# Attention scores from two float32r products on full stacks, with q and k loaded in token order

## The chip, the core and the metric

The program runs on one core of a Trainium2 chip. Its time is device time in microseconds (us), the median of several executions. The core has five engines with queues of their own: TensorE (PE, with its weight loads shown as PEld), VectorE (DVE), ScalarE (ACT), GpSimd (POOL) and SyncE (SP), which issues nearly all transfers here. Engines wait for each other by semaphores only; within an engine instructions go in the order in which they were issued.

## What is computed

Causal attention with a decay, over 4 batches of 8 heads, 576 tokens and 64 columns per head, then two feed-forward blocks over the 2304 tokens of width 512, with 2048 hidden columns each:

```python
log_f = np.log(np.clip(f, 0.0001, 1.0))
cum = np.cumsum(log_f, axis=-1)
scores = q @ k.T / sqrt(64) + cum[:, None] - cum[None, :]   # above the diagonal: -1e9
attn = exp(scores - max) ; attn = attn / (sum(attn) + 1e-9)
x = attn @ v                                    # heads side by side: 2304 x 512
h = x @ w_in  ; x = (h * tanh(softplus(h))) @ w_out          # first block
h = x @ w_in2 ; out = (h * cos(h)) @ w_out2                   # second block
```

The weights come as float64 and are cut into two float32r parts (`hi`, `lo`) on the chip; the feed-forward products take three float32r matmuls each (x high by weight high, x high by weight low, x low by weight high).

## The kernel before

**Attention.** The heads go in pairs, 16 of them: `jobs`. A pair of batch 0 is two jobs (query blocks 0 and 1, then 2 to 4), so batch 0 has eight small jobs; each pair of batches 1 to 3 is one full job of five blocks, twelve in all. A full job's blocks have 64, 128, 128, 128 and 128 query rows, and the keys seen by them (`w`) are 64, 192, 320, 448 and 576; the last is cut at 384, so that its products are 384 and 192 wide.

`load_job` (L401) loads q and k of a pair, a DMA each, so that one partition holds `C` neighbouring tokens. `prep_job` (L435) makes a *stack* of them: it transposes pieces of at most 96 tokens on TensorE (L462) into a bank of PSUM, and copies these to the stack by `ScalarE` (L474, both heads of k and the second head of q) and `VectorE` (L476, the first head of q). The copies write every `C`th column, which puts tokens back into order. A stack is `[128, head, q or k, token]` in float32: 64 rows of q or k, a row of the running sum `cum` and rows of 1 and -1, so that one product of 128 rows gives score plus decay. There are two stacks in a ring (`stk0`, `stk1`): the next job's is made in the last half-steps of the current job, from half-step `begin` on.

`scores` (L482) runs one float32 product for each head and cut (L491), and then on VectorE the mask and the row maximum in one reduction (L519), on ScalarE the exponential (L524); `normalise` (L530) divides on GpSimd (L538). Three blocks later `transposes` turns the result on TensorE (L565, L581) and `av` multiplies with v (L603) and cuts x into two float32r parts (L618, L619). The block of 64 rows holds both heads side by side, 64 columns of TensorE each, with a mask of its own (`mask2`).

**Feed-forward.** From the second batch on, steps of the first feed-forward pass (half of the hidden columns, tiles of 256 tokens, L205 and L227) are issued between the half-steps of attention. Behind attention come the rest of that pass, the other half of the columns and the second block, on tiles of 384 tokens.

**Order.** The text of the program gives priorities; the order on each engine is then made by a scheduler with a model of the chip before the program is compiled. Tiles of a tag are given out in turn from a pool with `bufs` buffers, and the taker of one waits until its last user is done.

Of the kernel before, what the change touches and what calls it, by code (L numbers as in the profile page):

```python
# [9 lines left out]
F32 = mybir.dt.float32  # L10
# [26 lines left out]
def tile_attention_two_ffn(  # L37
# [31 lines left out]
    rawp = ctx.enter_context(tc.tile_pool(name="raw", bufs=3))  # L69
# [3 lines left out]
    mask2 = const.tile([128, 320], F32, name="mask2")  # L73
# [6 lines left out]
    cumd = dram.tile([B * H, S], F32, name="cumd")  # L80
# [7 lines left out]
    def split_weights(layer, chunks, pool, slot0=0):  # L88
# [11 lines left out]
        def load(i):  # L100
            if i < len(pieces):
                c, nm, nb, nn, src, per, u, slot = pieces[i]
                raws[i] = rawp.tile([128, per, nn, 2], I32, tag="raw", name="raw")
                nc.sync.dma_start(out=raws[i].rearrange("p b n t -> p b (n t)"), in_=src[:, u : u + per])

        PF = 2
# [37 lines left out]
    def ffn_units(passes, p, hbank, abank, ready):  # L144
# [12 lines left out]
        def load_x(ti):  # L157
# [8 lines left out]
            t = p.tile([128, 2, NK, TB], F32R, tag="x", name="x")[:, :, :, 0:T]  # L166
# [126 lines left out]
        def v_1(n):  # L293
# [3 lines left out]
            t = tmp("n", n)  # L297
# [86 lines left out]
    def attention_units(p, bank):  # L384
# [16 lines left out]
        def load_job(jb):  # L401
# [32 lines left out]

        def prep_job(jb):  # L435
# [6 lines left out]
            src = cums[0][h0 : h0 + 2] if jb == 0 else cumd[h0 : h0 + 2]  # L442
            nc.sync.dma_start(out=st[96:97, :, 0], in_=src)
            nc.sync.dma_start(out=st[64:65, :, 1], in_=src)
# [14 lines left out]
            for g in groups:  # L459
# [3 lines left out]
                for which, lo in ((0, qlo), (1, 0)):  # L463
# [18 lines left out]
        def scores(jb, i):  # L482
# [352 lines left out]
```

## Time and profile before

| | us |
|---|---|
| median of the runs (3) | 1109.8 |
| lowest, highest | 1107.9, 1110.19 |
| the profiled execution | 1108.41 |
| its span | 1106.6 |
| TensorE busy | 1066.5 (96%) |
| VectorE busy | 642.2 (58%) |
| ScalarE busy | 588.6 (53%) |
| GpSimd busy | 230.4 (21%) |
| score products, L491 | 115.1 of records, 384 of them |

The mean granted clock was 0.991. Attention takes roughly the first 400 us, and the share of TensorE that is busy is lowest in the first slices of the span. Busy time of a matmul record includes its way through the array, so the sum of a line's records is more than the time for which the line holds TensorE; the distance between starts tells that. Rows are named `engine line out<-in`; `128x448` is partitions by elements.

### The profile page before, as it was taken

The page shows a single profiled execution, that of the slowest core. Times are in us where ns is not written, and L with a number is a line of the kernel's source. Part 1 is how long each engine was busy: PE and PEld are TensorE (multiplying, and loading weights), DVE is VectorE, ACT ScalarE, POOL GpSimd, SP SyncE. Part 2 cuts the span into 40 slices and gives each one's busy share as a digit, 9 for nine tenths or more (in the row PEclk, how much of TensorE's full clock was granted, in tenths as well). Part 3 has the DMA queues.
Part 4 walks back from the last instruction along what each step waited for, and adds up shares of the span by engine and source line. Part 5 has one row for each costly group of instructions (what it writes and reads, how often), then busy time and mean ns, then how long its engine had stood idle before and what let it go on. Part 6 is the DMA issues. An engine that isn't in the chain of part 4 may idle for free.

```text
span 1106.6 us, 17736 instructions
## 1 busy us (share of the span) xinstructions
PE 1066.5 (96%) x6496; PEld 936.6 (85%) x6496; DVE 642.2 (58%) x1461; ACT 588.6 (53%) x1196; POOL 230.4 (21%) x267
## 2 busy tenths in 40 slices
PE   5888999899999999999999999999999999999998
PEld 4565787578877879999999999879999999999997
DVE  6768775576656566453555625996445454454543
ACT  5776776767767655443444424665334343343433
POOL 6545632232322323130111101230000000000000
PEclk9899999999999999999999999999999999999999
DMA  7744622442232127463455544542001020100000
GB/s 163 183 122 126 196 55 74 110 130 54 74 91 93 33 73 228 158 210 114 158 190 185 168 153 142 172 134 67 20 30 57 1 86 1 58 29 1 30 1 29
DMA packets 118807, 110.53 MB, mean 100 GB/s; under 512 B 64560, under 2 KB 100912, under 8 KB 118720
## 3 DMA queue, kind: packets, MB, share of 16 engines
q1 hardware_dynamic: 118720, 109.40, 32.5%
q8 instruction: 51, 0.84, 0.3%
q14 instruction: 36, 0.29, 0.1%
HBM read 80.99 MB, written 28.39 MB: 99 GB/s over the span
## 4 chain that ended last, share of the span: by engine, by line
PE 83%; DVE 7%; ACT 5%; issue 3%; POOL 1%; DMA 1%; SPq 0%; ACTq 0%; POOLq 0%; DVEq 0%
PE h L205 19%; PE acc L236 17%; PE acc L227 16%; PE hx L205 14%; PE s L491 7%; PE s L603 5%; PE s L581 4%; ACT stk L474 3%; PE s L462 1%; DVE raw L123 1%; DVE raw L124 1%; DVE raw L133 1%; DVE s L519 1%; ACT s L524 1%; DMA raw<-in_moe_w_in_dram 0%
## 5 line engine op out<-in xcount | busy, mean ns | idle before, releaser
L205 PE MATMUL h<-x,wih 128*128 128x384 f32 (+1 forms) x1056 | 242.6, 317 | 0.0
L343 DVE TENSOR_TENSOR gl<-e,gh 128x384 fp32r<-128x384 f32 (+1 forms) x157 | 108.8, 693 | 142.5 <-ACT gh L335 142.5
L205 PEld LDWEIGHTS h<-x,wih 128*128 128x128 f32 x1056 | 180.9, 189 | 8.9 <-issue 2.8
L205 PE MATMUL h<-x,wil 128*128 128x384 f32 (+1 forms) x528 | 167.5, 317 | 0.0
L205 PE MATMUL hx<-x,wih 128*128 128x384 f32 (+1 forms) x672 | 166.2, 328 | 0.0
L335 ACT ACTIVATE gh<-e 128x384 fp32r<-128x384 f32 (+1 forms) x180 | 97.9, 545 | 100.6 <-DVE e L331 53.8
L227 PE MATMUL acc<-gl,woh 128*128 128x256 f32 (+1 forms) x480 | 148.9, 311 | 0.0
L227 PE MATMUL acc<-gh,woh 128*128 128x256 f32 (+1 forms) x480 | 148.5, 312 | 0.1
L227 PE MATMUL acc<-gh,wol 128*128 128x256 f32 (+1 forms) x480 | 147.5, 308 | 0.0
L491 PE MATMUL s<-stk 128*128 128x192 f32 (+7 forms) x384 | 115.1, 426 | 15.2 <-ACT stk L474 6.3
L538 POOL TENSOR_SCALAR s<-s,sm 128x448 f32<-128x448 f32 (+5 forms) x144 | 90.8, 645 | 159.7 <-DVE sm L536 50.4
L205 PEld LDWEIGHTS hx<-x,wih 128*128 128x128 f32 x672 | 120.1, 188 | 4.2
L236 PE MATMUL acc<-woh,gl 128*128 128x512 f32 x288 | 113.3, 397 | 3.1 <-DVE gl L343 3.1
L236 PE MATMUL acc<-wol,gh 128*128 128x512 f32 x288 | 113.7, 395 | 0.0
L236 PE MATMUL acc<-woh,gh 128*128 128x512 f32 x288 | 112.3, 390 | 0.8 <-DVE part L272 0.8
L205 PE MATMUL hx<-x,wil 128*128 128x384 f32 (+1 forms) x336 | 110.4, 328 | 0.0
L524 ACT ACTIVATE s<-s,mx 128x448 f32<-128x448 f32 (+5 forms) x144 | 83.1, 578 | 41.6 <-DVE mx L519 40.9
L205 PEld LDWEIGHTS h<-x,wil 128*128 128x128 f32 x528 | 99.8, 189 | 1.3 <-issue 0.6
L316 ACT ACTIVATE n<-n 128x384 f32<-128x384 f32 x96 | 50.4, 525 | 87.1 <-DVE n L305 87.1
L227 PEld LDWEIGHTS acc<-gh,woh 128*128 128x128 f32 x480 | 90.7, 190 | 2.8 <-issue 1.1
L227 PEld LDWEIGHTS acc<-gl,woh 128*128 128x128 f32 x480 | 90.9, 189 | 2.1 <-issue 0.7
L227 PEld LDWEIGHTS acc<-gh,wol 128*128 128x128 f32 x480 | 91.0, 190 | 2.0 <-issue 1.1
(88 smaller groups left out, 1705.0 us busy)
## 6 DMA issues: line engine op xcount, KB each, us to landing
raw<-in_moe_w_in_dram SPq DMA_DIRECT2D x32, 512.0 KB
raw<-in_moe_w_out_dram SPq DMA_DIRECT2D x32, 512.0 KB
x<-xd SPq DMA_DIRECT2D x6, 1536.0 KB
x<-yd SPq DMA_DIRECT2D x6, 1536.0 KB
x<-xd SPq DMA_DIRECT2D x8, 1024.0 KB
xd<-xs SPq DMA_DIRECT2D x12, 576.0 KB
natk<-in_k_dram SPq DMA_DIRECT2D x16, 288.0 KB
pd<-part SPq DMA_DIRECT2D x18, 256.0 KB
```

The lines of the kernel that those rows point to most:

```text
L205: nc.tensor.matmul(o, lhsT=a[wsl], rhs=b[:, kk, :], start=(kk == 0 and i == 0), stop=(kk == NK - 1 and i == 2),)
L227: nc.tensor.matmul(o, lhsT=a[dsl], rhs=b[:, gs], start=(start and i == 0 and d % nsub == 0), stop=(end and i == 2), skip_group_check=True,)
L236: nc.tensor.matmul(acc[ti][m], lhsT=a[:, ms], rhs=b[:, j, :], start=(start and i == 0), stop=(end and i == 2),)
L316: nc.scalar.activation(out=t, in_=t, func=AF.Sin, scale=TWO_PI)
L335: nc.scalar.activation(out=gh, in_=e, func=AF.Copy)
L343: marks["v1"] = nc.vector.tensor_tensor(out=gl, in0=st[n][0], in1=f(gst[n][0]), op=ALU.subtract)
L474: nc.scalar.activation(out=o, in_=i_, func=AF.Copy, scale=sc)
L491: marks["score"] = nc.tensor.matmul(o, lhsT=st[:, j, 0, qs], rhs=st[:, j, 1, c0:c1], start=True, stop=True)
L524: nc.scalar.activation(out=s[:, 0:w], in_=s[:, 0:w], func=AF.Exp, scale=-1.0, bias=mx, accum_out=sm[:, j : j + 1])
L538: nc.gpsimd.tensor_scalar(out=s[:, 0:w], in0=s[:, 0:w], scalar1=sm[:, j : j + 1], scalar2=1.0, op0=ALU.mult, op1=ALU.mult)
L581: nc.tensor.transpose(t[:, 128 * x : 128 * x + 128], ss[j][:, QS[c] : QS[c] + 128], ident)
L603: nc.tensor.matmul(t[64 * j : 64 * j + 64, c0:width], lhsT=vt[jb][0:kr, c, j], rhs=pt[0:kr, j, c, c0:width], start=(c == 0), stop=(c == nb ...
```

## The change

The stacks become float32r and have room for two parts, `x` = 0 and 1: `[128, q or k, x, head, token]`. Part 0 has 128 rows: the high part of q (or k) in rows 0 to 63 and, in rows 64 to 127, for q the high part again, for k the low part. Part 1 has 68 rows: for q the low part, for k the high part again, and four rows of ones and of `cum`, which is itself stored in two parts. Each score is the sum of two products in PSUM, one per part (L524).

Each piece in PSUM is now written to the stack four times by three engines: ScalarE writes the high part (L501), VectorE the low part as the piece times its scale less the high part (L502), and the high part again goes by ScalarE for the first head of q (L506) or by GpSimd from the stack (L508). q and k are loaded so that one partition holds every 96th token (two DMAs each, L417), so the pieces are contiguous in the stack; only job 0 keeps the old order. The block of 64 rows takes a product of 128 columns for each head, and its reduction is split in two (L560). The stacks take more room, which is found by fewer buffers: `raw` 2 (was 3), q and k 3 together (was 4), `n` 2 (was 3), the feed-forward's x tiles of 256 and of 384 tokens in tiles of their own. The preparation begins one half-step earlier.

```diff
@@ load_job
-                t = p.tile([128, 6, 2, D], F32, tag=f"nat{nm}", name=f"nat{nm}", bufs=2)
-                nc.sync.dma_start(out=t[0:P, 0:C], in_=src[b, hs, lo:khi].rearrange("h (p c) d -> p c h d", c=C))
+                t = p.tile([128, 6, 2, D], F32, tag="nat", name=f"nat{nm}", bufs=3)
+                if jb == 0:
...
+                else:
+                    for j in range(2):
+                        nc.sync.dma_start(
+                            out=t[0:P, 0:C, j], in_=src[b, 2 * hp + j, lo:khi].rearrange("(c p) d -> p c d", c=C)
+                        )
@@ prep_job
+                    sc = 0.125 if which == 0 else 1.0
                     for j in range(2):
-                        o = st[0:64, j, which, lo:khi].rearrange("r (p c) -> r c p", c=C)[:, c0 : c0 + n]
-                        i_ = t[64 * j : 64 * j + 64, at : at + n * P].rearrange("r (c p) -> r c p", p=P)
-                        sc = 0.125 if which == 0 else 1.0
-                        if which or j:
-                            nc.scalar.activation(out=o, in_=i_, func=AF.Copy, scale=sc)
+                        i_ = t[HALVES[j], at : at + n * P]
+                        if jb == 0:
+                            i_ = i_.rearrange("r (c p) -> r c p", p=P)
+
+                        def o(x, rows):
...
+                            return st[rows, which, x, j, lo + c0 * P : lo + (c0 + n) * P]
+
+                        again, low = (o(0, bottom), o(1, top)) if which == 0 else (o(1, top), o(0, bottom))
+                        nc.scalar.activation(out=o(0, top), in_=i_, func=AF.Copy, scale=sc)
+                        nc.vector.scalar_tensor_tensor(
+                            out=low, in0=i_, scalar=sc, in1=f(o(0, top)), op0=ALU.mult, op1=ALU.subtract
+                        )
+                        if which == 0 and j == 0:
+                            nc.scalar.activation(out=again, in_=i_, func=AF.Copy, scale=sc)
                         else:
-                            nc.vector.tensor_scalar(out=o, in0=i_, scalar1=sc, scalar2=None, op0=ALU.mult)
+                            nc.gpsimd.tensor_copy(again, f(o(0, top)))
@@ scores
-            def product(o, j, c0, c1):
-                marks["score"] = nc.tensor.matmul(
-                    o, lhsT=st[:, j, 0, qs], rhs=st[:, j, 1, c0:c1], start=True, stop=True
-                )
+            def product(o, j, c0, c1, cols=qs):
+                for x, rows in ((0, slice(0, 128)), (1, slice(0, 68))):
+                    marks["score"] = nc.tensor.matmul(
+                        o, lhsT=wide(st, rows, x, j, cols), rhs=st[rows, 1, x, j, c0:c1],
+                        start=x == 0, stop=x == 1,
+                    )
...
             if r == 64:
-                t = bank()[:, 0:w]
+                t, parts = None, []
                 for j in range(2):
-                    product(t[64 * j : 64 * j + 64], j, 0, w)
-                heads.append([(t, 0, w, mask2[:, 320 - w : 320])])
+                    if t is None or 2 * w > 512:
+                        t = bank()
+                    o = t[:, j * w : j * w + w] if 2 * w <= 512 else t[:, 0:w]
+                    product(o, j, 0, w, slice(QS[i] - 64 * j, QS[i] - 64 * j + 128))
+                    end = S - 64 + 64 * j
+                    parts.append((o, 0, w, maskt[:, end - w : end], HALVES[j]))
+                heads.append(parts)
@@ attention_units
-            ring.append(p.tile([128, 2, 2, S], F32, name=f"stk{i}", bufs=1))
+            ring.append(p.tile([128, 2, 2, 2, S], F32R, name=f"stk{i}", bufs=1))
...
-                begin = max(0, 2 * len(bl) - 5)
+                begin = max(0, 2 * len(bl) - 6)
```

On TensorE, before, the end of the sixth full job stands like this (`stk_99` is the stack in use, `stk_115` the next job's; `x2` counts like instructions in a row):

```order
L491 MATMUL s_2415<-stk_99 128x448
L491 MATMUL s_2417<-stk_99 128x448
L603 MATMUL s_2427<-p,natv 64x256 x8
L603 MATMUL s_2427<-p,natv 64x128 x2
L462 MATMUL s_2441<-ident,natq 128x96 x5
L565 MATMUL s_2474<-ident,s 64x128
L462 MATMUL s_2481<-ident,natq 128x96
L462 MATMUL s_2481<-ident,natk 128x96 x4
L491 MATMUL s_2506<-stk_99 128x384
L491 MATMUL s_2508<-stk_99 128x384
L491 MATMUL s_2510<-stk_99 128x192 x2
L462 MATMUL s_2525<-ident,natk 128x96 x2
```

The same place after the change (`stk_101` in use, `stk_108` the next):

```order
L482 MATMUL s_2710<-ident,natq 128x96 x5
L524 MATMUL s_2723<-stk_101 128x448 x2
L524 MATMUL s_2726<-stk_101 128x448 x2
L644 MATMUL s_2737<-p,natv 64x256 x8
L644 MATMUL s_2737<-p,natv 64x128 x2
L482 MATMUL s_2751<-ident,natq 128x96
L482 MATMUL s_2751<-ident,natk 128x96 x4
L606 MATMUL s_2794<-ident,s 64x128
L482 MATMUL s_2801<-ident,natk 128x96 x2
L524 MATMUL s_2825<-stk_101 128x384 x2
L524 MATMUL s_2828<-stk_101 128x384 x2
L524 MATMUL s_2831<-stk_101 128x192 x4
```

The first five transposes of q now stand ahead of the products of width 448, and the last two of k ahead of those of width 384 and 192, where they stood behind them; each product is two.

On ScalarE the evacuation of that job stood, before, as one run:

```order
L524 ACTIVATE s,sm<-s,mx 128x448 x2
L618 ACTIVATE xs<-s_2427 128x256
L474 ACTIVATE stk_115<-s_2441 64x5x96
L474 ACTIVATE stk_115<-s_2481 64x96
L474 ACTIVATE stk_115<-s_2481 64x4x96 x2
L474 ACTIVATE stk_115<-s_2525 64x2x96 x2
L524 ACTIVATE s,sm<-s,mx 128x576
```

After, exponentials (L565), a part of x (L659) and a copy of transposed rows (L598) stand between its pieces:

```order
L501 ACTIVATE stk_108<-s_2710 64x480
L659 ACTIVATE xs<-s_2737 128x256
L501 ACTIVATE stk_108<-s_2751 64x96
L501 ACTIVATE stk_108<-s_2801 64x192
L506 ACTIVATE stk_108<-s_2751 64x96
L501 ACTIVATE stk_108<-s_2751 64x96
L501 ACTIVATE stk_108<-s_2801 64x192
L501 ACTIVATE stk_108<-s_2751 64x384
L598 ACTIVATE p<-s_2858 128x2x2x128
L565 ACTIVATE s,sm<-s,mx 128x576
L501 ACTIVATE stk_108<-s_2751 64x384
L565 ACTIVATE s,sm<-s,mx 128x576
```

The six copies became nine, one of which stands ahead of these rows, and the next exponential of a whole row (128x576) stands between the last two of them.

On GpSimd, the divisions (L579, L538 before) of that stretch have the new copies among them:

```order
L508 CAST stk_108<-stk_108 64x480
L579 TENSOR_SCALAR s<-s,sm 128x448 x2
L508 CAST stk_108<-stk_108 64x96
L508 CAST stk_108<-stk_108 64x384
L508 CAST stk_108<-stk_108 64x192
L508 CAST stk_108<-stk_108 64x384
L508 CAST stk_108<-stk_108 64x192
L579 TENSOR_SCALAR s<-s,sm 128x576 x2
```

Before, that engine had only L538 and L341 there; now the last four copies of k go behind the division of the 448 wide block and ahead of that of 576.

## Rows read from the trace of the kernel before

**Rows 1.** Time by stage: PE, PEld, DVE, ACT, POOL busy (instructions), clock, DMA share, GB/s.

```profile
0.00:130.00 130.00, 105.71 (x663) 74.40 (x664) 97.31 (x267) 89.36 (x199) 78.68 (x99) 0.93 0.59 153
130.00:400.00 270.00, 262.75 (x1892) 207.70 (x1891) 166.95 (x532) 188.70 (x429) 80.56 (x117) 1.00 0.30 84
440.00:480.00 40.00, 40.00 (x335) 40.00 (x335) 19.61 (x30) 18.77 (x31) 11.25 (x8) 1.00 0.51 167
520.00:560.00 40.00, 40.00 (x232) 40.00 (x232) 20.72 (x32) 17.21 (x34) 5.42 (x5) 1.00 0.58 190
80.00:120.00 40.00, 36.43 (x248) 26.16 (x247) 35.49 (x88) 27.86 (x64) 27.05 (x26) 0.96 0.50 142
```

**Rows 2.** Instructions by line, L491: busy us, mean ns, idle before; then min/median/max ns.

```profile
L491 PE MATMUL s<-stk 128*128 128x448 f32 x64 | 30.6, 586 | 0.0
L491 PE MATMUL s<-stk 128*128 128x384 f32 x64 | 25.8, 501 | 2.9 <-ACT stk L474 0.9 <-DVE p L559 0.9 <-DVE xs L619 0.8
L491 PE MATMUL s<-stk 128*128 128x192 f32 x112 | 23.4, 332 | 0.1
...
L491 PE MATMUL s<-stk x384: 222/432/955, 9.3 to 393.8; 128*128 128x192 f32 x56, 128*128 128x448 f32 x32, 128*128 128x384 f32 x32, 128*64 128x64 f32 x24
```

**Rows 3.** Timeline of TensorE around L491: start us, busy us, work.

```profile
323.01 2.10 PE L491 MATMUL s<-stk 128*128 128x384 f32 x8
324.95 0.33 PE L462 MATMUL s<-ident,natk 96*128 96x96 f32 x2
...
334.75 1.67 PE L491 MATMUL s<-stk 128*128 128x448 f32 x4
336.35 0.65 PE L603 MATMUL s<-p,natv 64*64 64x256 f32 x4
```

**Rows 4.** Timeline at 321 us: TensorE's weight loads for L462.

```profile
321.03 0.45 PEld L462 LDWEIGHTS s<-ident,natq 96*128 96x128 f32 x5 [0.17 <-issue]
```

**Rows 5.** Groups by line and shape: VectorE, ScalarE, GpSimd (busy us, mean ns, idle before).

```profile
L476 DVE TENSOR_SCALAR stk<-s 64x480 f32<-64x480 f32 x12 | 12.4, 1037 | 0.5 <-PE s L462 0.5
...
L331 DVE SCALAR_TENSOR_TENSOR e<-n,h 128x384 f32<-128x384 f32 x48 | 26.5, 553 | 25.5 <-ACT n L316 25.5
...
L519 DVE CUSTOM_DVE_ANT_0 s<-s,maskt 128x192 f32<-128x192 f32 x24 | 7.5, 351 | 0.0
...
L474 ACT ACTIVATE stk<-s 64x480 f32<-64x480 f32 x12 | 12.7, 1062 | 10.7 <-DVE stk L476 10.7
...
L474 ACT ACTIVATE stk<-s 64x192 f32<-64x192 f32 x32 | 16.6, 520 | 1.8 <-PE s L462 1.3
...
L284 ACT ACTIVATE e<-h 128x384 f32<-128x384 f32 x24 | 11.7, 488 | 15.8 <-PE h L205 15.6
...
L284 ACT ACTIVATE e<-h 128x512 f32<-128x512 f32 x7 | 4.1, 589 | 3.2 <-PE h L205 3.2
...
L538 POOL TENSOR_SCALAR s<-s,sm 128x448 f32<-128x448 f32 x32 | 22.4, 711 | 32.3 <-DVE sm L536 21.8 <-PE s L462 9.7 <-PE s L581 0.8
...
L538 POOL TENSOR_SCALAR s<-s,sm 128x192 f32<-128x192 f32 x24 | 11.9, 507 | 2.5 <-ACT e L314 1.1 <-DVE sm L536 1.0 <-ACT p L557 0.3
```

**Rows 6.** TensorE's waits, 130 to 400 us; chain of waits, 195 to 203 us.

```profile
PE s L491 <- ACT stk L474: 2.3, 4, 0.9
...
by line: ACT stk L474 44.1%; PE s L603 16.5%; DVE stk L476 11.6%; PE s L581 8.4%; issue 7.3%; DVE xs L619 5.3%; ACT xs L618 4.9%; PE s L491 4.2%
```

**Rows 7.** Timeline at 99 us; L299 on VectorE by itself (min/median/max ns).

```profile
99.22 1.39 POOL L138 TENSOR_TENSOR wol<-raw,woh 128x512 fp32r<-128x512 f32 x1 [0.30 <-ACT woh L137]
...
99.38 0.32 DVE L476 TENSOR_SCALAR stk<-s 64x96 f32<-64x96 f32 x1
...
99.54 1.35 DVE L299 TENSOR_SCALAR n<-e 128x512 f32<-128x512 f32 x1
...
L299 DVE TENSOR_SCALAR n<-e x23: 408/427/1387, 61.1 to 412.0; 128x512 f32<-128x512 f32 x23
```

More of the change, by code (lines that the diff above doesn't have):

```diff
@@ L68, in tile_attention_two_ffn @@
     w0p = ctx.enter_context(tc.tile_pool(name="w0", bufs=1))
-    rawp = ctx.enter_context(tc.tile_pool(name="raw", bufs=3))
+    rawp = ctx.enter_context(tc.tile_pool(name="raw", bufs=2))
     ident = const.tile([128, 128], F32, name="ident")
     maskt = const.tile([128, S], F32, name="maskt")
-    mask2 = const.tile([128, 320], F32, name="mask2")
     two = const.tile([128, 1], F32, name="two")
@@ L79, in tile_attention_two_ffn @@
     pd = dram.tile([128, NK, NT], F32, name="pd")
-    cumd = dram.tile([B * H, S], F32, name="cumd")
+    cumd = dram.tile([B * H, 2, S], F32, name="cumd")
     W = {}
@@ L102, in load @@
                 c, nm, nb, nn, src, per, u, slot = pieces[i]
-                raws[i] = rawp.tile([128, per, nn, 2], I32, tag="raw", name="raw")
+                pl, nbuf = (late[0], 1) if late and i % 3 > 1 else (rawp, 2)
+                raws[i] = pl.tile([128, per, nn, 2], I32, tag="raw", name="raw", bufs=nbuf)
                 nc.sync.dma_start(out=raws[i].rearrange("p b n t -> p b (n t)"), in_=src[:, u : u + per])
-        PF = 2
+        PF = 2 if late else 1
         with tc.issue_after(marks["cum"].ins):
@@ L165, in load_x @@
             src = xd if tl["layer"] == 1 else yd
-            t = p.tile([128, 2, NK, TB], F32R, tag="x", name="x")[:, :, :, 0:T]
+            if attention_over:
+                t = late[0].tile([128, 2, NK, TB], F32R, tag="x", name="x", bufs=2)[:, :, :, 0:T]
+            else:
+                t = ap.tile([128, 2, NK, TA], F32R, tag="xa", name="xa", bufs=2)
             nc.sync.dma_start(
@@ L441, in prep_job @@
             h0 = b * H + 2 * hp
-            src = cums[0][h0 : h0 + 2] if jb == 0 else cumd[h0 : h0 + 2]
-            nc.sync.dma_start(out=st[96:97, :, 0], in_=src)
-            nc.sync.dma_start(out=st[64:65, :, 1], in_=src)
+            top, bottom = HALVES
+            for which, rows, lo in ((0, slice(64, 66), qlo), (1, slice(66, 68), 0)):
+                if jb == 0:
+                    for j in range(2):
+                        nc.sync.dma_start(
+                            out=f(st[rows, which, 1, j, lo:khi]), in_=cums[0][h0 + j : h0 + j + 1, :, lo:khi]
+                        )
+                else:
+                    nc.sync.dma_start(
+                        out=f(st[rows, which, 1, :, lo:khi]),
+                        in_=cumd[h0 : h0 + 2, :, lo:khi].rearrange("j x s -> x j s"),
+                    )
             if jb == 0:
@@ L511, in scores @@
                         product(o, j, c0, c1)
[L512 removed]
+                        heads[j].append((o, c0, c1, maskt[:, S - w + c0 : S - w + c1], None))
             ss = []
@@ L516, in scores @@
                 prev = None
-                for o, c0, c1, mk in parts:
-                    mx = new("mx", 6)
+                for o, c0, c1, mk, rows in parts:
+                    if rows is None or rows.start == 0:
+                        mx = new("mx", 6)
+                    rs = slice(0, 128) if rows is None else rows
                     marks["ttr"] = nc.vector.tensor_tensor_reduce(
-                        out=s[:, c0:c1], in0=o, in1=mk, scale=-1.0, scalar=BIG if prev is None else prev,
-                        op0=ALU.add, op1=ALU.min, accum_out=mx,
+                        out=s[rs, c0:c1], in0=o[rs], in1=mk[rs], scale=-1.0,
+                        scalar=BIG if prev is None else prev, op0=ALU.add, op1=ALU.min, accum_out=mx[rs],
                     )
-                    prev = mx
+                    prev = mx if rows is None else None
                 nc.scalar.activation(
@@ L694, in make_masks @@
         )
-        nc.gpsimd.memset(mask2, 0.0)
-        for x in (0, 64):
-            nc.gpsimd.affine_select(
-                out=mask2[x : x + 64, 256:320], in_=mask2[x : x + 64, 256:320], pattern=[[-1, 64]], base=0,
-                channel_multiplier=1, compare_op=ALU.is_ge, fill=MASKED,
-            )
     def decay_tables(p):
```

29 lines of the change are left out of this document (21 added, 8 removed).

## The prediction

> **What bounds the kernel now.** I read the time by stage first [rows 1]. In both 40 us stretches that I read behind the attention TensorE is busy 40.00 of 40 us, so only work taken from it would help there, and the change takes none. From 130 to 400 us (attention of batches 1 to 3, with the first feed-forward matmuls put between) it is busy 262.75 of 270: 7.25 us idle. VectorE has 166.95, ScalarE 188.70 and GpSimd 80.56 us of work there, 62%, 70% and 30%. In the first 130 us (batch 0) TensorE is busy 105.71 and VectorE 97.31; both wait for each other, and the granted clock is 0.93. The densest 40 us for VectorE are 80 to 120, with 35.49 busy. The last score product starts at 393.8 us [rows 2], so attention ends close to 400. So a microsecond of matmul saved after 130 us is worth nearly one, less new waits; before 130 us it is worth less.
>
> Then the score products at L491: 384 records, among them 64 of width 448, 64 of 384 and 112 of 192 [rows 2]. The program has 192 products, so a float32 product leaves two records. The timeline gives their spacing [rows 3]: from 323.01 the eight records are two products of 384 and two of 192; the next work on the engine starts 1.94 us later, and 1152 columns pass, 1.684 ns each. At 334.75 two products of 448 take 1.60 us with the switch of work, 1.79 ns per column. I use 1.684: 0.754 us at 448, 0.647 at 384, 0.539 at 320, 0.431 at 256, 0.323 at 192, 0.216 at 128.
>
> **Scores: what goes and what comes.** No row of before shows a float32r product narrower than 256, and wide ones stand in the stages that are full [rows 1]: 335 matmuls, of width 256, in 40.00 us (119.4 ns each) and 232, of 384, in 40.00 us (172.4 ns). The line through both is 13.4 ns plus 0.414 ns per column. Two such products per head: 0.398 us at 448, 0.345 at 384, 0.292 at 320, 0.239 at 256, 0.186 at 192, 0.133 at 128. Saved per product: 0.356, 0.302, 0.247, 0.192, 0.137, 0.083. The products of a full job (batches 1 to 3, both heads) are two each of 192, 320, 448, 384 and 192: 2 x (0.137 + 0.247 + 0.356 + 0.302 + 0.137) = 2.36 us, 28.3 in twelve jobs. Batch 0 has 8 each of 128, 256, 448, 384 and 192 (the code's blocks): 8.6. The blocks of 64 rows I cost at nothing: their two heads stood side by side in 64 columns each and now go one after the other at half the price per column. Sum for TensorE: -36.9.
>
> Below 256 the price has two ends: the line (0.414 ns per column) and the float32 price per record, 0.84 ns per column and product part, doubled again if a narrow float32r column takes four cycles (1.67 ns). I take the line, since nothing in the two points bends it; the other end is a rival.
>
> The change also puts many narrow products behind each other, each with its own load of 128 stationary columns. The transposes at L462 show such loads: five in 0.45 us from the start of the first to the end of the last, so at most 90 ns apart [rows 4]. That is less than the 93 ns that the line gives at width 192, so I add nothing. The Trainium skill ("TensorE: Matmul & The Clock Gate", LDWEIGHTS (loading the stationary operand)) puts a load at its columns divided by 1.2, 107 ns for 128. By that rule a matmul narrower than 226 columns could not go faster than 107 ns: 112 of width 192 would each lose 14 ns, 16 of 128 lose 41, and the saving would be 34.6 rather than 36.9; with the row's 90 ns at most it stays within 1 us of 36.9. The trace speaks against it here.
>
> **Evacuation of the transposed q and k.** Before, every piece went to the stack in one strided copy: ScalarE 1062 ns for 64x480 (L474), VectorE 1037 (L476, 32 of them) [rows 5]. After, in token order, each piece takes a `hi` on ScalarE (L501), a `low` on VectorE (L502), and a third copy on ScalarE (L506) or GpSimd (L508).
>
> ScalarE: no contiguous copy of 64 partitions stands in before; the nearest are L284, 488 ns at 384 columns and 589 at 512 [rows 5], 0.79 ns per column: 0.564 at 480, 0.336 at 192, 0.26 at 96. A full job had 1.06 + 0.38 + 2 x 0.88 + 2 x 0.52 = 4.2 us at L474 (480 and 192 from the rows [rows 5], 96 and 384 on the line through them, 96 near 0.38) and has 3 x 0.564 + 3 x 0.26 + 2 x 0.488 + 2 x 0.336 = 4.1. Nothing gained or lost in sum.
>
> VectorE: L331, the same operation with one input in PSUM, takes 553 ns at 384, and the reduction of L519, 351 at 192 [rows 5]: 1.05 ns per column between them, so 0.655 at 480, 0.25 at 96. The 136 new L502 are 24 of 480, 32 of 384, 8 of 320, 16 of 256, 32 of 192, 24 of 96: 61 us. The 32 L476 go: 12 of 480 (12.4 us [rows 5]), and 20 smaller ones that I scale to 9: -21.5. The blocks of 64 rows now reduce each head alone: 12 narrow ones at 0.3 and 4 of 320 at 0.57, estimates on the same line with the accumulator's read, +6. Sum +45.5 us, of which 2.57 in each full job (30.8) and 14.7 in batch 0. After 130 us VectorE stands then at about (166.95 + 30.8) / 270 = 73%, still below TensorE; the matmuls hide it. Were that cover gone, up to 30.8 us would show. In batch 0 it is 75% busy now and would be 86%, with TensorE waiting for it: I charge half of the 14.7, 7.4 us. The ends are 0 and 14.7.
>
> GpSimd: 104 copies (L508). No 64-row copy stands in before; L538 takes 711 ns at 448 and 507 at 192 [rows 5]: about 57 us by these, in an engine that is 30% busy after 130 us. Nothing by itself.
>
> **The wait at the boundary of two jobs.** TensorE's longest wait of 130 to 400 us is for L474, 2.3 us in 4 times [rows 6]; in the chain of waits from 195 to 203 us, across such a boundary, L474 has 44.1% and L476 11.6% [rows 6]. After, the last piece ends as `hi` (L501, 2 x 0.34 where L474 had 2 x 0.52), then VectorE's `low` beside GpSimd's copy, 0.51: +0.14 when GpSimd is free, and 0.85 when it has just begun an L538 of 0.71. Behind the waiting product stand the whole next block's reduction, exponential and transposes, but feed-forward matmuls are placed between as cover, and the preparation starts one half-step earlier. I take the middle, 0.5 a boundary, 12 x 0.5 = 6 us. The ends are 0 and 10.
>
> The smaller edits I cost at nothing: q and k loads in two DMAs instead of one and three shared buffers instead of four are issued a job ahead; one raw buffer less delays weight pieces that are wanted after 400 us; 72 matmuls of the last tile cover the load of the first late x tile. If that cover went, one such load would show, a few microseconds, inside the forecast's own range.
>
> **Sum.** -28.3 - 8.6 + 6 + 7.4 = -23.5. The profiled execution is 1108.4 (span 1106.6), so 1084.9; the median of the runs is 1109.8, 1.4 above it, so I predict 1086.
>
> **Rivals.**
> *A: no new waits.* TensorE's whole saving shows: 1109.8 - 36.9 = 1073. For it: 70% and 73% busy helpers and an earlier start. Against it: the chain of waits already runs through the evacuation.
> *B: VectorE and GpSimd get in each other's way.* At 99.22 a GpSimd operation on SBUF alone took 1.39 us, and L299 on VectorE beside it 1.35 us, where its median is 0.427 [rows 7]. L476, which reads PSUM, took 0.32 in the same stretch. `low` reads PSUM too, so it should come off as L476 did; L299, L343 and the others that read SBUF alone would not, and a chance of 13% is left. If each of the 104 copies adds 0.4 us to VectorE, it has 97.3 + 167.0 + 45.5 + 41.6 = 351.4 us of work; at the densest share it has shown, 35.49 of 40, that takes 396 us against 400 now: -4, so 1106. It turns slower than before from 0.43 us per copy. The Trainium skill ("SBUF — State Buffer", Who interferes with whom) has it that the two share one pair of SBUF ports, held by one of them at a time; L299 in [rows 7] agrees. By that rule each GpSimd copy would hold up VectorE's two-operand SBUF work beside it, which is the mechanism of B.
> *C: narrow float32r products are slow.* Under 256 columns four cycles per column instead of one, 1.67 ns: at 192 a pair costs 0.64 instead of 0.32 us, 56 x -0.32 = -17.9; at 128, 8 x -0.21 = -1.7; twelve blocks of 64 go from two products at 1.684 ns (0.22 us) to four at 1.67 (0.43), -2.5: -22.1 together. The widths from 256 on save 32 x 0.356 + 32 x 0.302 + 24 x 0.247 + 8 x 0.192 = 28.5. Net 6.4 saved, against 13.4 of waits and VectorE work: +7, so 1117. It decides from about 3.4 cycles per narrow column. For it: nothing narrow is in the trace; the attention's own narrow products there are all float32. Against it: the two float32r points lie on a line with next to no fixed cost.
>
> **How the numbers follow.** Forecast 54% (1077 to 1097 by the ends of its own waits), A 14%, B 13%, C 19%. A measurement of this kernel tells a change from none at about 0.2%, 2.2 us. Faster: 54 + 14 and 8 of B, 76%; within 0.2%: 4% of B; slower: C and the rest of B, 20%. The range goes from A's 1073 less 3, 1070, to B's and a little more, 1110; C is left out.
>
> **What would show it.** Right: L524 with 384 records, those of width 448 about 0.2 us apart and those of 192 about 0.09; attention's last transposes near 377 us rather than 400; L502 near 0.55 us at 384. Wrong: 192-wide products 0.3 us apart (C); L502 or L331 beside L508 at twice their length (B); TensorE idle well above 20 us between 130 and 380 us, waiting for L508 or L502 (then the boundary price was too low).

## The result and the profile after

The changed kernel takes 1125.6 us (median of 4 runs, 1121.0 to 1128.9) against 1109.6: a ratio of 1.0144, 95% interval [1.0106, 1.0182]. It is slower, where 1086 in a range of 1070 to 1110 had been forecast. The profiled execution took 1121.0 with a span of 1119.2 us, 12.6 more than before; it is the fastest of the four, and its mean granted clock was 0.977, that of the others 0.963 to 0.971.

The view by stage, columns as in [rows 1]:

```profile
0.00:130.00 130.00, 95.08 (x607) 74.09 (x608) 104.56 (x294) 82.98 (x209) 81.15 (x122) 0.91 0.47 125
130.00:400.00 270.00, 254.09 (x1881) 211.60 (x1881) 201.34 (x626) 188.01 (x476) 120.42 (x189) 0.96 0.34 95
```

Three things differ. VectorE has 34 us more work after 130 us. TensorE is idle 15.9 us there instead of 7.25. And the granted clock, 1.00 in that stretch before, is 0.96. (Up to its first clock record a trace counts the clock as full; for the first 130 us the view therefore stands too high, see below.) The last score product starts at 402.1 us instead of 393.8.

Each piece in PSUM is written to the stack three times: by L501, by L502, and by L506 or L508. The new operations themselves cost what the rows of before said (groups by line and shape):

```profile
L502 DVE SCALAR_TENSOR_TENSOR stk<-s,stk 64x384 fp32r<-64x384 f32 x32 | 17.8, 555 | 2.5 <-ACT stk L501 1.7
...
L334 DVE SCALAR_TENSOR_TENSOR e<-n,h 128x384 f32<-128x384 f32 x48 | 26.5, 552 | 28.0 <-ACT n L319 28.0
...
L501 ACT ACTIVATE stk<-s 64x480 fp32r<-64x480 f32 x24 | 13.5, 564 | 1.2 <-PE s L482 0.9
...
L508 POOL CAST stk<-stk 64x384 fp32r<-64x384 f32 x32 | 17.8, 556 | 15.2 <-ACT stk L501 15.0
```

L502 and L334 (L331 before) take 0.55 us at 384 columns: GpSimd's copies do not lengthen them, as rival B would have had it. Nor do they lengthen the work that reads SBUF alone by much: VectorE as a whole has 50.3 us more than before, where 45.5 had been estimated without B and 41.6 more with it. The 136 L502 sum to 62.2 us, 61 had been estimated.

The narrow products, from TensorE's timeline: four of 384, four of 192, each row followed by the next work.

```profile
160.25 0.87 PE L524 MATMUL s<-stk 128*128 128x384 f32 x4
160.96 0.40 PE L208 MATMUL h<-xa,wih 128*128 128x256 f32 x2
...
163.69 0.58 PE L524 MATMUL s<-stk 128*128 128x192 f32 x4
164.12 0.30 PE L208 MATMUL h<-xa,wil 128*128 128x256 f32 x1
```

Four of 384 take 0.71 us, 0.178 each (the line said 0.172); four of 192 take 0.43, 0.108 each (0.093). That is no price of four cycles per column: rival C is out, though its 1117 lies nearest to the time of all that was worked out.

TensorE's waits in the first 130 us (us in total, times, longest), and then the chain of waits from 38 to 60 us:

```profile
PE s L524 <- DVE stk L502: 18.0, 6, 4.7
PE s L482 <- DMA natq<-in_q_dram: 4.2, 1, 4.2
```

```profile
by line: DVE s L560 23.3%; DVE stk L502 15.8%; DVE raw L133 9.0%; DVE raw L123 8.0%; issue 7.6%; DVE raw L124 5.9%; DVE xa L660 5.4%; PE s L482 3.9%; PE s L622 3.9%; DVE p L600 3.1%; ACT s L565 3.0%; PE s L524 2.7%; ACT woh L137 2.5%; ACT s
```

In batch 0 the chain is for 70% VectorE's now: the small jobs follow each other too fast for the `low` parts. The first full job starts at 113.2 us instead of 104.5, with the same 120 feed-forward matmuls behind it. After 130 us it is different; the longest waits there (130 to 420 us) are for L598's copies and L560's reductions, and those for L502 come to 2.9 us:

```profile
PE s L524 <- ACT p L598: 3.1, 6, 0.7
PE s L524 <- DVE mx L560: 3.0, 5, 1.3
PE s L482 <- DVE stk L502: 2.0, 3, 0.7
...
PE s L524 <- DVE stk L502: 0.9, 1, 0.9
```

And the clock around a boundary of two jobs: the longest gap there, and the view by stage (the granted clock is the third column from the end):

```profile
335.09 0.30 PE L524 MATMUL s<-stk 128*128 128x64 f32 x1 [0.75 <-ACT p L598]
```

```profile
334.00:337.90 3.90, 2.91 (x18) 1.93 (x17) 3.46 (x12) 2.60 (x6) 0.76 (x2) 1.00 0.96 257
337.90:344.70 6.80, 6.80 (x31) 4.75 (x30) 2.26 (x14) 2.84 (x9) 2.37 (x5) 0.50 0.96 307
```

TensorE is idle for 1 us in the first stretch (one gap of 0.75 us, waiting for a copy of L598), and in the next 6.8 us it is granted half the clock, 1.2 GHz, and is busy all the time. There are 23.9 us of this between the start of the full jobs and the end of attention; before the change there were 3.2, right at the start of the first full job, and none after it.

Also the first 37.5 us run at the lower level (19.0 before). There is no clock record there yet; the spacing of the matmuls shows it. Four transposes in a row, early and late:

```profile
24.55 1.08 PE L622 MATMUL s<-ident,s 128*128 128x128 f32 x4
...
333.72 0.63 PE L622 MATMUL s<-ident,s 128*128 128x128 f32 x4
```

Counted so, 61 of the first 130 us are at the lower level, 36 before.

**A sum that closes.** At the lower level work takes up to twice as long (the 128-column transposes stand 0.213 us apart in the first 37 us and 0.109 later; the feed-forward products of 256 columns 0.213 instead of 0.120). So a span divides into TensorE's busy time counted at the full clock, half of the busy time that lies in low stretches (what the clock costs, by this estimate a little too high), and idle time. That it closes is by its making; it shows where the time went. From the records of TensorE, the low stretches and the span, for one profiled execution of each kernel on which the argument rests:

| us | busy, at full clock | clock | idle | span |
|---|---|---|---|---|
| before | 1053.0 | 13.6 | 40.1 | 1106.6 |
| changed | 1024.3 | 33.5 | 61.4 | 1119.2 |
| e1 products alone | 1018.5 | 49.4 | 47.8 | 1115.7 |
| e2 evacuation alone | 1055.6 | 16.3 | 50.1 | 1122.0 |
| e3 no low parts | 1021.3 | 21.2 | 57.7 | 1100.2 |
| e7 batch 0 as before | 1028.1 | 39.6 | 49.8 | 1117.5 |
| e8 products, early preparation | 1022.0 | 34.0 | 48.3 | 1104.2 |
| e9 late stack | 1052.7 | 23.5 | 42.6 | 1118.8 |
| e11 one part | 998.1 | 25.0 | 59.6 | 1082.7 |
| e12 token order | 1052.0 | 10.8 | 33.6 | 1096.3 |
| e13 two products, short copies | 1024.4 | 14.3 | 48.8 | 1087.5 |
| e14 token order, early preparation | 1051.3 | 15.3 | 36.7 | 1103.3 |

The change saved 28.7 us of TensorE's work, and gave back 19.9 by the clock and 21.3 by waits. Executions of one kernel differ in the clock (e1 below: up to 12 us of time), so a few microseconds in the clock column of two kernels are no difference.

### The profile page after: what moved, and what is told of

It reads as the page before. It is cut to its first block, busy times and chain, and to the rows that moved or that the text cites. A ratio compares the mean times of both kernels' runs of the same rounds, so it can differ in the third digit from the quotient of the medians.

```text
span 1119.2 us, 18191 instructions
## 1 busy us (share of the span) xinstructions
PE 1057.8 (95%) x6496; PEld 949.3 (85%) x6496; DVE 692.5 (62%) x1597; ACT 584.4 (52%) x1261; POOL 274.3 (25%) x365
## 4 chain that ended last, share of the span: by engine, by line
PE 75%; DVE 10%; DMA 5%; issue 4%; ACT 4%; POOL 2%; SPq 1%; ACTq 0%; DVEq 0%; POOLq 0%
PE h L208 18%; PE acc L239 17%; PE acc L230 14%; PE hx L208 13%; PE s L644 4%; PE s L622 4%; PE s L524 3%; DMA raw<-in_moe_w_out_dram 3%; DVE s L560 2%; DVE stk L502 1%; DVE raw L133 1%; DVE raw L124 1%; PE s L482 1%; DMA xd<-xs 1%; ACT s L565 1%
## 5 line engine op out<-in xcount | busy, mean ns | idle before, releaser
L208 PE MATMUL hx<-x,wih 128*128 128x384 f32 (+1 forms) x640 | 160.3, 330 | 0.0
L208 PE MATMUL h<-x,wih 128*128 128x384 f32 (+1 forms) x640 | 158.6, 330 | 0.0
L524 PE MATMUL s<-stk 68*128 68x192 f32 (+13 forms) x384 | 90.6, 343 | 31.7 <-DVE stk L502 19.0
L208 PEld LDWEIGHTS hx<-x,wih 128*128 128x128 f32 x640 | 115.1, 188 | 4.2
L208 PEld LDWEIGHTS h<-x,wih 128*128 128x128 f32 x640 | 115.1, 188 | 4.0
L579 POOL TENSOR_SCALAR s<-s,sm 128x448 f32<-128x448 f32 (+5 forms) x144 | 90.6, 642 | 108.4 <-DVE sm L577 59.3
L208 PE MATMUL h<-x,wil 128*128 128x384 f32 (+1 forms) x320 | 105.9, 331 | 0.0
L208 PE MATMUL hx<-x,wil 128*128 128x384 f32 (+1 forms) x320 | 105.8, 331 | 0.0
L524 PEld LDWEIGHTS s<-stk 128*128 128x128 f32 (+1 forms) x384 | 61.8, 206 | 44.6 <-DVE stk L502 15.6
L565 ACT ACTIVATE s<-s,mx 128x448 f32<-128x448 f32 (+5 forms) x144 | 83.3, 579 | 30.2 <-DVE mx L560 26.0
```

The lines of the kernel that those rows point to most:

```text
L208: nc.tensor.matmul(o, lhsT=a[wsl], rhs=b[:, kk, :], start=(kk == 0 and i == 0), stop=(kk == NK - 1 and i == 2),)
L524: marks["score"] = nc.tensor.matmul(o, lhsT=wide(st, rows, x, j, cols), rhs=st[rows, 1, x, j, c0:c1], start=x == 0, stop=x == 1,)
L565: nc.scalar.activation(out=s[:, 0:w], in_=s[:, 0:w], func=AF.Exp, scale=-1.0, bias=mx, accum_out=sm[:, j : j + 1])
L579: nc.gpsimd.tensor_scalar(out=s[:, 0:w], in0=s[:, 0:w], scalar1=sm[:, j : j + 1], scalar2=1.0, op0=ALU.mult, op1=ALU.mult)
```

## The experiments

Theories: **W**, the saving is real and the evacuation turns it into waits; **P**, the products are worth little by themselves; **C**, gaps in TensorE's work bring the lower clock, and that takes the saving (not rival C of the prediction). V, G and R are explained where an expectation brings them in.

**e1, the products alone.**

```diff
 (the kernel before, with its stack in float32r)
-                    o, lhsT=st[:, j, 0, qs], rhs=st[:, j, 1, c0:c1], start=True, stop=True
+                for x, rows in ((0, slice(0, 128)), (1, slice(0, 68))):
...
+                        rhs=st[rows, 1, j, c0:c1], start=x == 0, stop=x == 1,
```

> The kernel before with only the products changed: each score by two float32r products of its old stack (the second of 68 rows) and the 64-row blocks by one 128-wide product per head, evacuation and loads as before. The score is thereby roughly doubled. Theory W (the saved TensorE time is real, and the new evacuation turns it into waits and lower clock): 1080 to 1090 us against 1109.6. Theory P (two narrow float32r products save little, since none is faster than some 0.11 us and each change between float32 and float32r costs): 1100 to 1110.

Measured 1117.0 us (10 runs, 1108.5 to 1120.7), ratio 1.0058 [1.0033, 1.0083]: outside both. With no new work on the other engines but 6.5 us on VectorE (the reductions of the 64-row blocks, split as in the change), the cheaper products made the kernel slower. Batch 0 gained (first full job at 98.5 us), and then 68 us of attention ran at the lower level; the whole stretch, and the boundary near 201 us:

```profile
130.00:400.00 270.00, 259.21 (x1832) 213.05 (x1831) 167.88 (x536) 183.69 (x419) 81.70 (x115) 0.91 0.30 82
...
197.00:201.20 4.20, 3.03 (x23) 2.04 (x20) 2.73 (x8) 3.29 (x5) 1.04 (x2) 1.00 0.40 106
201.20:214.90 13.70, 13.55 (x53) 10.02 (x54) 5.59 (x25) 7.94 (x23) 2.55 (x5) 0.50 0.38 77
```

A gap of 1.08 us ahead of the transposes of L591 (the trace shows no releaser for it; before, the gap at this place was 0.85 us) and then 13.7 us at half the clock. Within this kernel the span goes with the clock: 1106.8 us at a mean of 0.975, 1118.9 at 0.961, 7.5 us per 0.01 over the ten runs.

**e2, the evacuation alone.**

```diff
-                for x, rows in ((0, slice(0, 128)), (1, slice(0, 68))):
...
+                    o, lhsT=f(wide(st, rows, 0, j, cols)), rhs=f(st[rows, 1, 0, j, c0:c1]), start=True, stop=True
```

> The changed kernel with one float32 product of part 0 in place of the two float32r products (part 1, so the decay and a cross term, is left out of the score); evacuation, loads and buffers as changed. Theory W: TensorE has its old work again on top of the new waits, so 1120 to 1140 us, but the granted clock between 130 and 400 us goes back to 1.00, since TensorE is idle less. Theory P: within 5 us of the changed kernel's 1125.6, since the products hardly differ.

Measured 1122.0, ratio 1.0124 [1.0100, 1.0147], and the clock between 130 and 400 us is 1.00:

```profile
130.00:400.00 270.00, 263.69 (x1884) 209.16 (x1884) 208.58 (x623) 187.29 (x470) 125.55 (x190) 1.00 0.34 94
```

The new evacuation costs 12.7 us by itself (15.4 by the profiled spans). The forecast's 13.4 of waits was near this, but not in its parts: nearly the whole loss lies in batch 0. The first full job starts at 117.7 us instead of 104.5, and from there to the last score product it takes 290.4 us, where it took 289.3 before. With its old work on TensorE, the evacuation of a full job is covered. The time lies in W's range; in P's too, so that it doesn't tell these two apart.

**e3, no low parts from the seventh job on.**

```diff
-                        nc.vector.scalar_tensor_tensor(
+                        if jb < 6:
+                            nc.vector.scalar_tensor_tensor(
```

> The changed kernel without the low parts on VectorE (L502) from the seventh job on; the low rows keep what earlier jobs left there. About 46 us less VectorE work in 14 jobs and one step less in the chain at each job's end. Theory W with VectorE as the place: 1095 to 1110 us, and TensorE's idle time after 130 us back to about 7 us. Theory P: 1120 or more. A third theory, that the clock alone costs the time: faster only as far as the granted clock rises, 1110 to 1118.

Measured 1105.5 (10 runs), ratio 0.9977 [0.9958, 0.9996]: W's range, 20 us less than the changed kernel. But idle time fell by 3.7 us only (11.0 us are left between 130 and 400, where W had about 7) and TensorE's work by 3; the clock gave 12.3. So `low` is a place where the time is lost, and most of what it costs comes by way of the clock. The profiled execution is the fastest of the ten here, so that 12.3 may be more than the usual.

**e4, filler matmuls in the waits of batch 0.**

```diff
+                    for _ in range(3):
+                        nc.tensor.matmul(t[:, 0:256], lhsT=ident, rhs=maskt[:, 0:256], start=True, stop=True)
```

> The changed kernel with three float32 matmuls of 256 columns that nobody reads put ahead of the first product of each of the eight jobs of batch 0, where TensorE waits 2 to 5 us for L502 (some 1.3 us of work at the full clock). Theory C (a good part of the loss is the clock, which falls after such waits): the granted clock of 0 to 130 us rises from 0.91 to 0.94 or more and the time falls by 4 to 10 us, to 1116 to 1121. Without an effect of the clock the fillers cost 0 to 10 us: 1125 to 1135.

Measured 1146.4, ratio 1.0342 [1.0289, 1.0394]. It missed on both sides. The view has the granted clock of the first 130 us at 0.82 instead of 0.91, but here the first clock record comes at 9.0 us and there at 37.5; with the time ahead of it counted as low, 57 of the 130 us are at the lower level instead of 61. The first full job starts at 121.1 us instead of 113.2, and from there to the end of attention 51.8 us are at the lower level instead of 23.9, where no filler stands. Why is not shown. This way of keeping the clock up failed and says nothing on the cause.

**e5, feed-forward steps spread more thinly.**

```diff
-            credit += min(1.0, max(0.15, 0.65 * (usable - issued) / until[0]))
+            credit += min(1.0, max(0.15, 0.45 * (usable - issued) / until[0]))
```

> The changed kernel with the feed-forward steps spread more thinly over the attention of batches 1 to 3 (factor 0.45 in place of 0.65 on the steps that are open), so that the jobs at the end of a batch, which now have none beside them, keep some. Theory C (TensorE's short waits bring the lower clock, and that takes the saving): the low stretches at 210 to 235 and at 338 us shrink, time 1112 to 1121 us. Theory V (the work of VectorE in the evacuation is the bound by itself): 1121 to 1130, since no VectorE work goes.

Measured 1134.0, ratio 1.0215 [1.0198, 1.0232], outside both: 37.5 us at the lower level in attention instead of 23.9. The jobs at the end of batch 1 still had no feed-forward work beside them (384 matmuls were issued by 218 us, as by 192 in the changed kernel), and the earlier jobs had less.

**e6, preparation from the second half-step on.**

```diff
-                begin = max(0, 2 * len(bl) - 6)
+                begin = max(0, 2 * len(bl) - 9)
```

> The changed kernel with the preparation of the next full job begun at the second half-step of a job's ten rather than the fifth. If the chain at the job boundary (transposes, L501, L502, L508, next product) is what TensorE waits for after 130 us: 1105 to 1116 us, with TensorE's idle time there down from 16 to 18 us to 10 or less and with it the low clock. If the waits come from VectorE's amount of work inside a job: no change, 1121 to 1130.

Measured 1120.5, ratio 1.0100 [1.0077, 1.0122]: below the second range by half a microsecond, far from the first. TensorE's idle time between 130 and 400 us is 13.6 us instead of 15.9: the boundary is not the main place of the waits there; they lie inside the jobs, too. In batch 0, where the edit changes nothing in the program's text, 75 of the first 130 us were at the lower level instead of 61, which is not explained and took part of the gain.

**e7, batch 0 as before.**

```diff
+                        if jb < 2 * NP:
+                            if which or j:
+                                nc.scalar.activation(out=o(0, top), in_=i_, func=AF.Copy, scale=sc)
...
+                if jb < 2 * NP:
...
+                        o, lhsT=st[:, 0, 0, j, qs], rhs=st[:, 1, 0, j, c0:c1], start=True, stop=True
```

> The changed kernel with batch 0 as before in what it computes (one float32 product, one copy of each piece by ScalarE or VectorE, no low parts) and batches 1 to 3 as changed. The trace has the changed kernel 8.7 us behind at the end of batch 0. Theories C and V both give back these 8.7 us: 1113 to 1119. If the loss in batch 0 is from the loads and buffers (two DMAs, one raw buffer fewer): 1121 to 1127.

Measured 1118.7, ratio 1.0083 [1.0061, 1.0105]. The first full job starts at 105.6 us: the loss of batch 0 came back, as expected, 7 us of it in the time, so that the fewer buffers and the split loads, which e7 keeps, cost 1 us there at most. The other 9 lie behind batch 0, where in the profiled execution 46 us were at the lower level.

**e8, the products alone with early preparation.** The kernel of e1 with

```diff
-                begin = max(0, 2 * len(bl) - 5)
+                begin = max(0, 2 * len(bl) - 8)
```

> The run of the products alone (old stacks and evacuation, two float32r products) with the preparation of the next full job begun at half-step two of ten rather than five. That run had 68 us at the lower clock after gaps of 0.6 to 1.7 us at the job boundaries. Theory C: with the gaps gone the clock stays up and the time falls from 1117 to 1083 to 1095. If the float32r products themselves bring the lower clock, not the gaps: 1112 to 1120, with 40 us or more at the lower clock.

Measured 1104.5, ratio 0.9951 [0.9932, 0.9970]. 12.5 us less than e1. The clock gave it (49.4 to 34.0 in the table); TensorE is idle as long as in e1. It stays 9 us above the range of theory C: gaps of 1.5 to 2 us remain at 154, 196 and 216 us, each with a low stretch behind it.

**e9, the stack late on purpose, products as before.**

```diff
-                            nc.scalar.activation(out=o, in_=i_, func=AF.Copy, scale=sc)
+                            for _ in range(2 if jb >= 2 * NP and g is groups[-1] else 1):
+                                nc.scalar.activation(out=o, in_=i_, func=AF.Copy, scale=sc)
```

> The kernel before with the last two copies of each stack (L474, 64x192) made twice in the twelve full jobs: float32 products, and the stack ready some 1.0 us later at each job boundary. Theory G (a gap of about a microsecond in TensorE's work brings the lower clock, whatever the products are): low stretches appear between 130 and 400 us, 20 us of them or more, and the time rises by 8 to 25 us, to 1118 to 1135. Theory R (it takes the cheaper float32r products too): none or one low stretch there, the time rises by the waits alone, 3 to 12 us, to 1113 to 1122.

Measured 1121.0, ratio 1.0109 [1.0094, 1.0124]. Between 130 and 400 us there are two low stretches, 13.7 us, where the kernel before has none:

```profile
205.00:208.80 3.80, 2.28 (x14) 1.50 (x14) 2.01 (x6) 3.73 (x9) 0.00 (x0) 1.00 0.90 180
208.80:215.60 6.80, 6.62 (x26) 4.18 (x27) 2.18 (x14) 3.12 (x10) 2.61 (x5) 0.50 0.00 0
```

So gaps bring the lower clock with float32 products as well, which R denied but for one stretch; but less than the 20 us that G named, and the time fits either. Both were partly wrong. Some gaps cost no clock: the kernel before, at the same boundary, has TensorE busy 2.12 of 3.40 us and keeps 1.00:

```profile
198.70:202.10 3.40, 2.12 (x14) 1.33 (x12) 0.98 (x6) 3.34 (x7) 0.00 (x0) 1.00 0.96 268
202.10:208.90 6.80, 6.80 (x45) 4.57 (x46) 4.55 (x22) 5.12 (x15) 2.56 (x5) 1.00 0.34 66
```

What exactly decides is open.

**e10, GpSimd's copies on ScalarE.**

```diff
-                            nc.gpsimd.tensor_copy(again, f(o(0, top)))
+                            nc.scalar.activation(out=again, in_=i_, func=AF.Copy, scale=sc)
```

> The changed kernel with the 104 copies of GpSimd (L508) made by ScalarE from PSUM instead. If GpSimd's copies hold up VectorE or end late: 1110 to 1120 us. If they are covered: ScalarE has some 45 us more work in attention and the time stays or rises, 1124 to 1140.

Measured 1158.6, ratio 1.0456 [1.0433, 1.0479], dearer than either range: TensorE idle 77.0 us, and a mean clock of 0.953. ScalarE has 43 us more work; GpSimd was the cheap place. That ScalarE stands in the chain of every block is the likely reason, which was not taken apart.

**e11, one part, short copies.** The kernel of e8 with one float32r product per score, the decay's sum in two rows, and the loads of the change, so that the copies are contiguous:

```diff
-                for x, rows in ((0, slice(0, 128)), (1, slice(0, 68))):
...
+                    rhs=st[:, 1, j, c0:c1], start=True, stop=True,
...
+                            o = st[0:64, which, j, lo + c0 * P : lo + (c0 + n) * P]
```

> The old stack in float32r with one float32r product per score (no low parts, so the score has the precision of one float32r part; the sum of the decay in two rows), q and k in token order with contiguous copies by ScalarE and VectorE, preparation from the third half-step on. VectorE has its old work, ScalarE about 25 us less, TensorE about 55 us less than before. If the waits stay as in the runs with the old evacuation and the clock falls with them: 1080 to 1100 us. If the clock takes all of it: 1100 to 1112.

Measured 1083.7, ratio 0.9764 [0.9748, 0.9781]. It gives up the low parts, so it is not the same computation, but shows what the work of TensorE is worth when little else is added: 55 us of it gone, 25 of the time (19 of them against e14, its like with float32 products).

**e12, token order alone.** The kernel before with the loads and contiguous copies of the change, float32 products:

```diff
+                        nc.sync.dma_start(
+                            out=t[0:P, 0:C, j], in_=src[b, 2 * hp + j, lo:khi].rearrange("(c p) d -> p c d", c=C)
+                        )
...
-                        o = st[0:64, j, which, lo:khi].rearrange("r (p c) -> r c p", c=C)[:, c0 : c0 + n]
+                            o = st[0:64, j, which, lo + c0 * P : lo + (c0 + n) * P]
```

> The kernel before with q and k loaded in token order by two DMAs each and the copies to the stack contiguous; products, parts and buffers as before. ScalarE's copies should take about half as long (64x480 from 1.06 to 0.56 us). TensorE's waits for L474 after 130 us are 2.3 to 4 us in all, so at most 2 to 6 us of gain: 1104 to 1109; if the smaller DMAs come late, 1110 to 1115.

Measured 1098.5, ratio 0.9904 [0.9889, 0.9919]: more than expected. L484 (L474 before) takes 567 ns for 64x480 instead of 1062, TensorE's idle time falls by 6.5 us, and no stretch of attention after batch 0 is at the lower level:

```profile
L484 ACT ACTIVATE stk<-s 64x480 f32<-64x480 f32 x12 | 6.8, 567 | 6.8 <-DVE stk L486 6.7
```

```profile
130.00:400.00 270.00, 267.92 (x1939) 212.31 (x1937) 167.61 (x530) 175.74 (x431) 83.06 (x118) 1.00 0.30 82
```

This is the fastest kernel here that keeps the whole precision of the score, and it beats the kernel before and the changed one.

**e13, two products on short copies.** The kernel of e11 with the two products of e1.

```diff
-                    rhs=st[:, 1, j, c0:c1], start=True, stop=True,
+                for x, rows in ((0, slice(0, 128)), (1, slice(0, 68))):
...
+                        rhs=st[rows, 1, j, c0:c1], start=x == 0, stop=x == 1,
```

> The run with one float32r part (token order, contiguous copies, early preparation) with two float32r products per score instead of one, as many and as wide as in the changed kernel; the score is roughly doubled. The work of TensorE at the full clock is some 30 us less than with one float32 product (1098.5 us). Theory C (the saving is real where the stack comes in time): 1083 to 1094 us. If the products are worth little by themselves, or their lighter work brings the lower clock anyway: 1095 to 1110.

Measured 1089.5, ratio 0.9830 [0.9807, 0.9854], C's range. It has no low parts either. Against e1 the evacuation is shorter and begins earlier (and the decay's sum stands in two rows), and the same products now gain: TensorE's work at the full clock is 1024.4 us as in the changed kernel, the clock costs 14.3 us instead of 49.4, and attention has a single low stretch of 3.4 us:

```profile
130.00:400.00 270.00, 260.21 (x2023) 219.26 (x2021) 179.63 (x564) 181.66 (x442) 84.17 (x120) 1.00 0.31 92
```

It is not less idle in all (48.8 us, 47.8 in e1 and 48.3 in e8): its gaps in the full jobs are at most 1.3 us long, where those of e1 and e8 reach 1.7 and 2.0. That their length makes the difference is not shown; e9 has low stretches with none above 1.3.

**e14, token order and early preparation.** The kernel of e12 with

```diff
-                begin = max(0, 2 * len(bl) - 5)
+                begin = max(0, 2 * len(bl) - 8)
```

> The run with token order alone (float32 products) with the preparation begun at the third half-step instead of the sixth. TensorE's waits for L484 there are 1.2 us after 110 us, so 1096 to 1099 us; if the transposes of the next job now stand in the way of the current one, 1099 to 1104.

Measured 1102.6, ratio 0.9948 [0.9927, 0.9968]: 4 us worse than e12, the second branch. So beginning earlier is no gain of itself, and e13's 1089.5 stands 13 us below its like with float32 products.

## Why the prediction was wrong

- **The step that failed: "a microsecond of matmul saved after 130 us is worth nearly one, less new waits".** TensorE's saving was counted at the full clock throughout. Work was saved (28.7 us), but TensorE, with more gaps in its work, was granted the lower level for longer, which cost 19.9 us in the profiled execution; the forecast had nothing for that. [rows 1] showed the granted clock at 0.93 where TensorE waits and at 1.00 where it does not, and that was passed over. Shown: e1, slower with hardly anything but cheaper products; e13, the same products faster with as much idle time but a clock that stays up; e9, low stretches made by late stacks alone. Which gaps bring the lower level stays open.
- **The saving was sized at 36.9; it was 28.7.** A product of 192 columns stands 0.108 us from the next rather than 0.093, and those of 64 columns 0.111, so the blocks of 64 rows lost (four products, 0.44 us, where two took 0.27 side by side) rather than cost nothing: 112 x 0.015 + 12 x 0.17, and 16 x 0.04 at 128, is 4.4 us of the 8.2. The rest is not attributed. A line through two points could not show such a floor. The loads of [rows 4] do follow each other faster, the transposes that they belong to at 0.082 us; what failed was to take this for the score products. The Trainium skill's rule ("TensorE: Matmul & The Clock Gate", LDWEIGHTS (loading the stationary operand)) gives an estimate of 107 ns for 128 columns. It agrees with the spacing of the score products, 0.108 and 0.111 us, and not with that of the transposes.
- **The waits were sized at 13.4; they are 21.3.** Batch 0: TensorE idle 9.3 us more up to its end, where 7.4 had been put; after it 9.9 more up to the end of attention instead of 6, and inside jobs as well as at their boundaries (e6). In batch 0 the mechanism, VectorE's added work and one more step in the chain, was right: TensorE waits 18.0 us for L502 there, and e7 gives the time back. Behind batch 0 it was not: from the first full job to the last score product TensorE was idle 8.1 us before, 6.8 with the new evacuation alone (e2), 14.5 with the cheaper products alone (e1) and 18.0 with both. There the gaps come with the cheaper products (likely because these cover less of the work beside them), so the saving and the waits cannot be priced apart.
- **The terms of the other engines held**: VectorE +50.3 us busy against +45.5 forecast, ScalarE -4.2 against 0, GpSimd +43.9 against +57.
- **Rivals.** A would have needed the waits to stay. B is out (L502 and L334 at 0.55 us, VectorE's sum, and e10). C is out by the spacing of narrow products; that its time was near is chance. None of the rivals had the clock in it.
- **"q and k loads in two DMAs" cost nothing** was right, and too modest: the contiguous copies that they allow are the one part of the change that gains alone, 10.5 us (e12).

## What to carry to other kernels

When work is taken from TensorE, ask what gaps this opens and look at the granted clock behind them: until the operations beside it are shorter too, the saving can be lost to a lower clock, as in e1. Shorten the chain that feeds the engine first (here the strided copies, 1%), then its own work (another 0.8% in e13, which leaves out the low parts). Take a change apart into its parts early: of the three here one gained 10 us, one lost 12, and one lost or gained depending on the others.

## What the runs showed of the hardware

- Executions of one program differ in the granted clock, and the time follows: in e1, from 1106.8 us at 0.975 to 1118.9 at 0.961. The kernel before, with few gaps, keeps to 0.988 to 0.996 in all runs.
- Behind gaps that add up to 0.7 to 2.6 us, TensorE was granted 1.2 GHz in the full jobs for 3.4 to 13.7 us, even when it was fully busy in that stretch. Not every such gap did it (e9, e12).
- A trace has no clock record at its start: TensorE ran at the lower level there (transposes 0.213 us apart) until the first one, at 19.0 us before the change and 37.5 after, while the view counts that time as full.
- Float32r products below 256 columns, with 128 stationary columns each, stood 0.108 us apart at 192 columns and 0.111 at 64, where the line through the wide ones gives 0.093 and 0.040.
- ScalarE's copies from PSUM took 564 to 567 ns for 64x480 into a contiguous row of the stack, and 1062 with a step of six columns.
